# MLP1 of an attention and two-MLP kernel in blocks of 256 and 384 tokens, with the wide blocks' sums packed in three PSUM banks

## The chip, the cores and the metric

The kernel runs on one core of a Trainium2 chip. The metric is the device time of one execution in microseconds (us), lower is better. The engines are named as in the profile: PE is TensorE (matmuls), PEld its weight loads, DVE is VectorE, ACT is ScalarE, POOL is GpSimd, SP issues the DMAs. PSUM has eight banks; one bank holds 512 fp32 values on each of 128 partitions.

## The reference

Windowed attention over 4 sequences of 576 positions (8 heads of 64), then two MLPs over all 2304 tokens (512 -> 2048 -> 512):

```
scores = scale * q @ k.T + slope_h * (-|i - j|), masked to 0 <= i - j < 128
attn   = softmax(scores) @ v
x      = attn with the heads side by side        # 2304 x 512
h = x @ w_in;  g = where(h >= 1, h, where(h <= -1, 0, (h + 1)**2 / 4));  x = g @ w_out
h = x @ w_in2; g = h * clip(h + 3, 0, 6) / 6;                            out = g @ w_out2
```

The weights come as 64-bit floats. slope_h is 2 to the power -(h + 1), scale is 1/8.

## The kernel before

**Numbers in two parts.** Each fp32 operand of a matmul is split in a high part (`split_hi`) and a remainder (`split_lo`), and a product is three matmuls (low x high, high x low, high x high) in `fp32r`. Every matmul names its stationary operand, and the trace has one weight load on PEld for each matmul.

**Attention.** The tokens are cut in `units`: (256, 320) for the first, third and fourth sequence, (192, 256, 128) for the second. A head of a unit is prepared once (`prep`: high and low part of k, q and v, with the 128 keys before the unit), and each 128 queries of it are a step with four stages (`stage_a` scores and exponential, `stage_b` transposes, `stage_c` the product with v, `stage_d` for the first three units). `tick` runs one stage of several steps. There are 160 steps, eight heads times 20, and 164 ticks. In a step the scores go to bank s, the transposes to t and t2 in turn, the product with v to r.

**MLP1** runs in nine blocks of 256 tokens. For each of 16 slices f of d_ff, `Mlp.first` makes h (12 matmuls with 256 columns), `activate` makes g in two parts (DVE, ACT, DVE, ACT, POOL), and `Mlp1.second` adds g times w_out to the sum (12 matmuls with 256 columns). The sum of a block, four pieces of 128 x 256, fills two banks (acc0, acc1). `Chunks.run` keeps `lag` slices between first and second: two, and four (`LAG_TAIL`) for the last two blocks. The first two blocks run in halves of 8 slices, in the order first half of 0, first half of 1, second half of 0, second half of 1. The hook of `spread` puts the ticks of attention between the slices: 20 before MLP1, 44 within blocks 0 and 1, then 12, 24, 24, 16 and 24 in blocks 2 to 6. So attention ends with block 6. Blocks 7 and 8 run in turns slice by slice (`tail_hook`), while the second MLP's weights are loaded and converted (`Weights.conv1` to `conv3`: two ACT passes, three DVE passes, one ACT copy, one DVE subtraction, each of 128 x 1024). A block's sum leaves PSUM in `finish`, and goes to x2d in HBM.

**MLP2** takes two blocks of 384 tokens in turns and then three of 512. Its `second` has 512 columns in a matmul, whatever the block.

**Order.** The queues of SP are in the order of the program. On the other engines a scheduler sets the order, close to that of the program; each engine executes its own queue in order.

**Start.** `make_consts` builds a distance table and a mask on POOL, and `make_bias` one bias table of 128 x 256 for each of the eight heads on DVE. In the first three units a column of ones beside v gives the softmax sum; POOL writes those ones (L258) again for every pair of heads, after the last reader of that buffer. `keep_busy` puts matmuls on zeros between the first steps, to keep PE active.

Of the kernel before, what the change touches and what calls it, by code (L numbers as in the profile page):

```python
# [39 lines left out]
def tile_window_attention_two_mlps(  # L40
# [28 lines left out]
    N1 = 256  # L69
    blocks1 = [(a, min(N1, NT - a)) for a in range(0, NT, N1)]  # L70
# [13 lines left out]
    assert needs[:3] == [1, 2, 3]  # L84

# [11 lines left out]
    def keep_busy(bank, n):  # L97


        nc.tensor.matmul(bank[:, :n], zeros[:, :P], zeros[:, :n], start=True, stop=True, skip_group_check=True)  # L100

    rel_mask = []

    def make_consts():
        both = cpool.tile([P, 2, PIECE], F32, tag="m", name="both")
        irel, mask = both[:, 0, :2 * P], both[:, 1, :2 * P]
        rel_mask.extend((irel, mask))

        nc.gpsimd.iota(irel, pattern=[[-1, 2 * P]], base=P, channel_multiplier=1,
                       allow_small_or_imprecise_dtypes=True)  # L110
        nc.gpsimd.memset(mask, 0.0)
        nc.gpsimd.affine_select(out=mask, in_=mask, compare_op=ALU.is_ge, fill=NEG / scale,
                                base=P, pattern=[[-1, 2 * P]], channel_multiplier=1)
        nc.gpsimd.affine_select(out=mask, in_=mask, compare_op=ALU.is_ge, fill=NEG / scale,
                                base=WINDOW - 1 - P, pattern=[[1, 2 * P]], channel_multiplier=-1)
        make_identity(nc, ident)

    def make_bias(h):
        nc.vector.scalar_tensor_tensor(out=bias8[:, h, :], in0=rel_mask[0], scalar=-slopes[h] / scale,
                                       in1=rel_mask[1], op0=ALU.mult, op1=ALU.add)  # L120
# [116 lines left out]
    class Attention:  # L237
# [4 lines left out]

        def load(self, n):
# [40 lines left out]
        def prep(self, n):  # L284
# [27 lines left out]

        def stage_a(self, n, i):

            u = heads[n]
            if n < H and i == 0:
                make_bias(n)
# [9 lines left out]
            if u.whole:  # L327
                keep_busy(ps, BANK if u.unit == 0 else 2 * P)
            nc.tensor.matmul(ps[:m, :nk], u.qs[:, qo:qo + m], u.kh[:, ko:ko + nk], start=True, stop=False)  # L329
            nc.tensor.matmul(ps[:m, :nk], u.qs[:, qo:qo + m], u.kl[:, ko:ko + nk], start=False, stop=True)  # L330
# [4 lines left out]
                out=pt[:m, :nk], in0=ps[:m, :nk], in1=bias8[:m, u.h, bo:bo + nk], scale=-scale,  # L335
# [10 lines left out]
        def stage_b(self, n, i):  # L346
# [10 lines left out]
            bank = psum.tile([P, BANK], F32, tag=("t", "t2")[(n * 3 + i) % 2], name=f"t{n}_{i}")  # L357
# [113 lines left out]
        def to_x(self, u, xf, e_lo):  # L471
            a, end = u.t0, u.t0 + u.nq
            while a < end:
                blk = a // N1
                e = min(end, (blk + 1) * N1)
                src = xf[:, a - u.t0:e - u.t0]
                hi, lo = (self.xs[blk][:, p, u.h // 2, a - blk * N1:e - blk * N1] for p in range(2))
                split_hi(HI["x"], hi, src)
                split_lo(e_lo, lo, src, hi)
                a = e  # L480
# [62 lines left out]
    class Mlp1(Mlp):  # L543
        acc_tags = [("acc0", "acc1")]
        n_block = 0
        lag = LAG

        def accs(self, n):
            tags = self.acc_tags[self.n_block % len(self.acc_tags)]
            self.n_block += 1  # L550
            return [psum.tile([P, BANK], F32, tag=tags[i], name=f"acc{i}") for i in range(-(-KC * n // BANK))]
# [12 lines left out]
        def second(self, acc, g, f, n, first, last):  # L564

            per = BANK // n
            for e in range(KC):
                i, o = divmod(e, per)
                for k, (a, b) in enumerate(((1, 0), (0, 1), (0, 0))):
                    nc.tensor.matmul(acc[i][:, o * n:(o + 1) * n], self.W.w_out(a, f)[:, e * P:(e + 1) * P], g[:, b, :n],  # L570
                                     start=(first and k == 0 and o == 0), stop=(last and k == 2),
                                     skip_group_check=True)
# [12 lines left out]
        def finish(self, acc, t0, n, more):  # L585

            m = BANK // n * n
            o = self.left if more else self.opool.tile([P, 2, PIECE], F32, tag="m", name="o1")
            for i, (ps, hbm) in enumerate(zip(acc, self.places(acc, t0, n))):
                if more:  # L590
                    nc.vector.tensor_tensor(out=o[:, i, :m], in0=ps[:, :m], in1=o[:, i, :m], op=ALU.add)
                else:
                    split_hi(("act", "dve")[i % 2], o[:, i, :m], ps[:, :m])
                nc.sync.dma_start(out=hbm, in_=o[:, i, :m].rearrange("p (e t) -> p e t", t=n))

    class Mlp2(Mlp):
        g_lo = "g2"
        banks = ("acc0", "acc1", "r", "s", "t", "t2")
# [72 lines left out]
    def split_x2(pool, xs, j, c, raw):  # L671
# [16 lines left out]
    halves = {}  # L688
    W1 = Weights("a", w_in1, w_out1, cpool)
# [14 lines left out]
    def run_block(mlp1, j, part, hook):  # L704
        for f in part:
            chunks.run(mlp1, j, f, part, xs[j], lambda: hook(f, 0), lambda: hook(f, 1))

    with ExitStack() as actx:
        mlp1 = Mlp1(W1, blocks1, actx.enter_context(tc.tile_pool(name="r", bufs=2)),
                    actx.enter_context(tc.tile_pool(name="g", bufs=LAG + 1)))  # L710
# [15 lines left out]
        new_x(1)
# [8 lines left out]

        new_x(2)
# [21 lines left out]
        new_x(3)  # L758
        run_block(mlp1, 1, Z, spread(Z, 4, KF))
        for j in range(2, len(blocks1) - 2):  # L760
            new_x(j + 2)
# [5 lines left out]
    chunks.flush()  # L767
    opool = ctx.enter_context(tc.tile_pool(name="o", bufs=5))
# [100 lines left out]
```

## Time and profile before

| | us |
|---|---|
| three timed runs | 1011.0, 1012.44, 1012.46 (median 1012.44) |
| the profiled execution | 1012.21 |
| its span, first to last instruction | 1010.4 |
| PE busy | 981.5 |
| DVE, ACT, POOL busy | 600.4, 520.1, 250.4 |

The last matmul of MLP1 is followed by the first of MLP2 at 609.88 us of the span. A matmul's record runs from its start to a modelled end, and the records of neighbours overlap. The pace is therefore read from start to start, and the mean of a record is longer than the step. A span of 1010.4 within 1012.21 leaves 1.8 us ahead of the first and behind the last instruction.

### The profile page before, as it was taken

How to read it: one execution, taken by the hardware profiler on the slowest of the kernel's cores; microseconds unless marked ns; L12 is line 12 of the kernel's file. 1: busy time of each engine (PE TensorE's matmuls, PEld its weight loads, DVE VectorE, ACT ScalarE, POOL GpSimd, SP SyncE). 2: the span in 40 equal slices, each digit the busy share in tenths (PEclk: the TensorE clock that was granted, in tenths of full speed). 3: DMA queues.
4: the chain of work that ended last, by engine and by line, in shares of the span. 5: the costliest groups of instructions: out<-in, count | busy, mean ns of one | idle time of the engine just before them, and what ended most of it. 6: DMA issues, size and time to landing. Idle time of an engine off the chain costs nothing.

```text
span 1010.4 us, 18091 instructions
## 1 busy us (share of the span) xinstructions
PE 981.5 (97%) x6454; PEld 889.2 (88%) x6454; DVE 600.4 (59%) x1584; ACT 520.1 (51%) x1286; POOL 250.4 (25%) x398
## 2 busy tenths in 40 slices
PE   7899999999899999999999999999999999999998
PEld 4678888999899999999999998999988888888886
DVE  5789996576687776677658987922242223222222
ACT  4678885455677766666636867422232223122221
POOL 4325464444556555555400000000000000000000
PEclk9799999999999999999999999999999999999999
DMA  6575823212222212212006655000020002001001
GB/s 179 165 219 172 263 80 100 77 54 54 82 75 78 79 46 71 68 54 75 2 22 209 222 181 202 1 1 1 1 104 1 1 1 84 1 0 42 1 1 42
DMA packets 69786, 78.52 MB, mean 78 GB/s; under 512 B 7488, under 2 KB 61760, under 8 KB 69696
## 3 DMA queue, kind: packets, MB, share of 16 engines
q1 hardware_dynamic: 69696, 77.36, 24.7%
q8 instruction: 51, 0.84, 0.3%
q14 instruction: 39, 0.32, 0.1%
HBM read 66.85 MB, written 10.49 MB: 77 GB/s over the span
## 4 chain that ended last, share of the span: by engine, by line
PE 83%; DVE 5%; DMA 3%; ACT 3%; issue 3%; POOL 1%; SPq 1%; ACTq 0%; POOLq 0%; DVEq 0%
PE h L530 36%; PE acc L623 20%; PE acc L570 17%; PE r L449 2%; PE s L329 2%; PE t L363 1%; PE s L330 1%; PE t L364 1%; PE r L394 1%; DMA kr<-kT 1%; DMA rawa<-w_out 1%; DVE ma L179 1%; DVE wa L134 1%; SPq L251 1%; DVE p L334 1%
## 5 line engine op out<-in xcount | busy, mean ns | idle before, releaser
L530 PE MATMUL h<-x,wa 128*128 128x256 f32 x1728 | 240.6, 286 | 2.4 <-DVE sm L340 1.3
L570 PE MATMUL acc<-g,wa 128*128 128x256 f32 x1728 | 236.6, 285 | 1.4 <-POOL g L134 1.3
L530 PEld LDWEIGHTS h<-x,wa 128*128 128x128 f32 x1728 | 220.3, 192 | 4.0 <-DVE sm L340 1.5
L570 PEld LDWEIGHTS acc<-g,wa 128*128 128x128 f32 x1728 | 217.9, 191 | 3.4 <-POOL g L134 1.8
L530 PE MATMUL h<-x,wb 128*128 128x512 f32 (+1 forms) x960 | 210.5, 368 | 1.2 <-DVE r L613 1.2
L623 PE MATMUL acc<-wb,g 128*128 128x512 f32 x864 | 209.4, 390 | 0.0
L530 PEld LDWEIGHTS h<-x,wb 128*128 128x128 f32 x960 | 176.2, 188 | 26.5 <-DVE r L613 1.5
L623 PEld LDWEIGHTS acc<-wb,g 128*128 128x128 f32 x864 | 161.7, 188 | 32.4
L613 DVE SCALAR_TENSOR_TENSOR r<-r,h 128x512 f32<-128x512 f32 (+1 forms) x80 | 50.7, 633 | 203.4 <-ACT r L612 203.4
L612 ACT ACTIVATE r<-h 128x512 f32<-128x512 f32 (+1 forms) x80 | 44.4, 555 | 211.5 <-PE h L530 211.4
L127 ACT CAST g<-r 128x256 fp32r<-128x256 f32 (+2 forms) x224 | 104.4, 466 | 86.1 <-DVE r L613 50.1
L134 POOL TENSOR_TENSOR g<-r,g 128x256 fp32r<-128x256 f32 x112 | 88.9, 794 | 129.9 <-ACT g L127 122.5
L558 ACT ACTIVATE r<-r 128x256 f32<-128x256 f32 x144 | 60.1, 417 | 78.8 <-DVE r L557 75.3
L134 DVE TENSOR_TENSOR g<-r,g 128x512 fp32r<-128x512 f32 (+2 forms) x112 | 64.5, 576 | 46.6 <-ACT g L127 46.5
L337 ACT ACTIVATE p<-p,sm 128x256 f32<-128x256 f32 (+2 forms) x160 | 76.1, 477 | 23.0 <-DVE sm L334 19.8
L559 DVE TENSOR_TENSOR r<-h,r 128x256 f32<-128x256 f32 x144 | 60.6, 421 | 29.9 <-ACT r L558 28.8
L557 DVE TENSOR_SCALAR r<-h 128x256 f32<-128x256 f32 x144 | 60.4, 419 | 28.8 <-PE h L530 24.0
L134 POOL TENSOR_TENSOR qs<-qr,qs 64x256 fp32r<-64x256 f32 (+3 forms) x72 | 66.5, 924 | 28.7 <-issue 10.8
L334 DVE CUSTOM_DVE_ANT_0 p<-s,bias 128x256 f32<-128x256 f32 (+2 forms) x160 | 59.8, 374 | 13.1 <-PE s L330 12.3
L329 PE MATMUL s<-kh,qs 128*128 128x256 f32 (+2 forms) x160 | 56.7, 356 | 5.0 <-POOL qs L134 3.6
L342 POOL TENSOR_SCALAR p<-p,sm 128x256 f32<-128x256 f32 (+2 forms) x104 | 48.0, 461 | 54.4 <-DVE sm L341 35.2
L376 DVE TENSOR_TENSOR tl<-t,th 128x256 fp32r<-128x256 f32 (+2 forms) x120 | 41.7, 348 | 11.7 <-ACT th L127 10.3
(75 smaller groups left out, 1124.5 us busy)
## 6 DMA issues: line engine op xcount, KB each, us to landing
rawa<-w_in SPq DMA_DIRECT2D x16, 512.0 KB, 5.2
rawa<-w_out SPq DMA_DIRECT2D x16, 512.0 KB, 4.8
rawb<-w_in SPq DMA_DIRECT2D x16, 512.0 KB, 3.7
rawb<-w_out SPq DMA_DIRECT2D x16, 512.0 KB, 4.7
x2d<-o SPq DMA_DIRECT2D x22, 256.0 KB, 2.5
kr<-kT SPq DMA_DIRECT2D x48, 112.0 KB, 2.6
out<-o SPq DMA_DIRECT2D x18, 256.0 KB, 2.1
kr<-kT SPq DMA_DIRECT2D x64, 64.0 KB, 2.3
```

The source lines that it names most:

```text
L127: nc.scalar.copy(hi, x)
L134: engines[eng].tensor_tensor(out=lo, in0=x, in1=hi.bitcast(F32), op=ALU.subtract)
L329: nc.tensor.matmul(ps[:m, :nk], u.qs[:, qo:qo + m], u.kh[:, ko:ko + nk], start=True, stop=False)
L334: nc.vector.tensor_tensor_reduce(out=pt[:m, :nk], in0=ps[:m, :nk], in1=bias8[:m, u.h, bo:bo + nk], scale=-scale, scalar=3.0e38, op0=ALU.ad ...
L337: nc.scalar.activation(out=pt[:m, :nk], in_=pt[:m, :nk], func=AF.Exp, bias=sm[:m, 0:1], scale=-1.0, accum_out=None if u.whole else sm[:m, ...
L530: nc.tensor.matmul(ps[:, :n], self.W.w_in(a, c, f), self.x_chunk(x, b, c, n), start=(k == 0), stop=(k == 3 * KC - 1))
L557: nc.vector.tensor_scalar(out=r[:, :n], in0=ps[:, :n], scalar1=-1.0, scalar2=1.0, op0=ALU.max, op1=ALU.min)
L558: nc.scalar.activation(out=r[:, :n], in_=r[:, :n], func=AF.Square, bias=0.5, scale=0.5)
L559: nc.vector.tensor_tensor(out=r[:, :n], in0=ps[:, :n], in1=r[:, :n], op=ALU.max)
L570: nc.tensor.matmul(acc[i][:, o * n:(o + 1) * n], self.W.w_out(a, f)[:, e * P:(e + 1) * P], g[:, b, :n], start=(first and k == 0 and o == 0 ...
L613: nc.vector.scalar_tensor_tensor(out=r[:, :n], in0=r[:, :n], scalar=1.0, in1=ps[:, :n], op0=ALU.min, op1=ALU.mult)
L623: nc.tensor.matmul(acc[t][:, :DM], g[:, b, t * P:(t + 1) * P], self.W.w_out(a, f), start=(first and k == 0), stop=(last and k == 2))
```

## The change

- MLP1: three blocks of 256 and then four of 384 tokens. The sum of a block of 384 is four pieces of 128 x 384, and a bank takes one such piece and 128 columns more. In blocks 3 to 5 (`packed`) the fourth piece is cut in three of 128 columns, one behind the piece in each of three banks (acc0, acc1, t2). So its 3 matmuls are 9 in each slice.
- The last block (6) is alone, without packing: four banks (s, t, acc0, acc1) for the sum, h0 and r for h, with a lag of two slices. The `flush` ahead of it and ahead of MLP2 is gone.
- Attention: (256, 320), (192, 256, 128), (256, 128, 192), (192, 256, 128). Steps stay 160, but the heads are 88 instead of 72. The ticks are 20, 24, 32 and 24 in blocks 2 to 5. From the fourth block's units on the transposes use bank t alone.
- The x of MLP1 is one tile in two halves with a place for each block, instead of three buffers.
- One table of distances for all heads: k is scaled by scale / slope_h in `prep`, and the slope comes in with the minimum on DVE. The 8 DVE instructions of `make_bias` go.
- The ones beside v are written once, ahead of all loads. ACT writes one column of the zeros at the start, which loads its function table then. `keep_busy` uses matmuls of 256 columns.
- The conversion of the second weights is spread differently (0.5 a slice of the last block, then 0.6 a slice of each MLP2 block).

```diff
-    N1 = 256
-    blocks1 = [(a, min(N1, NT - a)) for a in range(0, NT, N1)]
+    N1, WIDE = 256, 384
+    assert (NT - 3 * N1) % WIDE == 0
+    blocks1 = [(a, N1) for a in range(0, 3 * N1, N1)] + [(a, WIDE) for a in range(3 * N1, NT, WIDE)]
...
-        for n in (192, 256, 128) if b == 1 else (256, 320):
+        for n in ((256, 320), (192, 256, 128), (256, 128, 192), (192, 256, 128))[b]:
...
+            unit = scale / slopes[u.h]
+            assert math.frexp(unit)[0] == 0.5
+            nc.scalar.activation(out=u.kh[:, :nk], in_=u.kr[:, :nk], func=AF.Copy, scale=unit)
...
+            nc.vector.scalar_tensor_tensor(out=u.kl[:, :nk], in0=u.kr[:, :nk], scalar=unit,
+                                           in1=u.kh[:, :nk].bitcast(F32), op0=ALU.mult, op1=ALU.subtract)
...
-            bank = psum.tile([P, BANK], F32, tag=("t", "t2")[(n * 3 + i) % 2], name=f"t{n}_{i}")
+            bank = psum.tile([P, BANK], F32, tag=("t", "t2")[(n * 3 + i) % 2] if u.unit <= first_wide else "t",
+                             name=f"t{n}_{i}")
...
+        acc_tags = ("acc0", "acc1", "t2")
+        packed = True
...
+            return [psum.tile([P, BANK], F32, tag=self.acc_tags[i], name=f"acc{i}")
+                    for i in range(-(-KC // (BANK // n)) - (self.packed and n == WIDE))]
...
             per = BANK // n
             for e in range(KC):
-                i, o = divmod(e, per)
+                if e == len(acc) and per == 1:
+
+                    pieces = [(i, n, i * P, P) for i in range(n // P)]
+                else:
+                    pieces = [(e // per, e % per * n, 0, n)]
                 for k, (a, b) in enumerate(((1, 0), (0, 1), (0, 0))):
...
+                    for i, o, t, m in pieces:
+                        nc.tensor.matmul(acc[i][:, o:o + m], self.W.w_out(a, f)[:, e * P:(e + 1) * P],
+                                         g[:, b, t:t + m], start=(first and k == 0 and o == 0),
+                                         stop=(last and k == 2), skip_group_check=True)
...
-    chunks.flush()
-    opool = ctx.enter_context(tc.tile_pool(name="o", bufs=5))
...
+    mlp1.tags = ("h0", "r")
+    mlp1.acc_tags = ("s", "t", "acc0", "acc1")
+    mlp1.packed = False
...
     for f in FULL:
-        chunks.run(mlp1, y, f, FULL, xs[y], lambda: None, tail_hook(f, False))
-        chunks.run(mlp1, z, f, FULL, xs[z], lambda: None, tail_hook(f, True))
-    chunks.flush()
-    for f in range(KF - behind, KF):
-        W2.load()
-        W2.load()
...
+        chunks.run(mlp1, z, f, FULL, z, lambda: None, lambda: tail_hook(f))
```

Three places show how the instructions move. The first is PE in a slice whose sum was 2 banks before (top), and in a packed slice of block 3 (below); h is the product with w_in, acc the sum, wa the weights of MLP1:

```order
L530 MATMUL h<-x,wa_1363 128x256 x12
L570 MATMUL acc_3061<-g,wa_1119 128x256 x6
L570 MATMUL acc_3062<-g,wa_1119 128x256 x6
L449 MATMUL r_3353<-th_3225,vs_2750 128x128
L449 MATMUL r_3353<-tl_3226,vs_2750 128x128
```

```order
L549 MATMUL h<-x,wa_776 128x384 x12
L598 MATMUL acc_4313<-g,wa_647 128x384 x3
L598 MATMUL acc_4314<-g,wa_647 128x384 x3
L598 MATMUL acc_4315<-g,wa_647 128x384 x3
L598 MATMUL acc_4313<-g,wa_647 128x128
L598 MATMUL acc_4314<-g,wa_647 128x128
L598 MATMUL acc_4315<-g,wa_647 128x128
L598 MATMUL acc_4313<-g,wa_647 128x128
L598 MATMUL acc_4314<-g,wa_647 128x128
L598 MATMUL acc_4315<-g,wa_647 128x128
L598 MATMUL acc_4313<-g,wa_647 128x128
```

(two more rows of 128 columns follow.) The fourth piece of the sum has become nine matmuls of 128 columns in a row.

The second is PE where MLP1 hands over to MLP2 (x_0 and x_1 are the first two blocks of MLP2, wb its weights), before and then now:

```order
L570 MATMUL acc_8491<-g,wa_2233 128x256 x6
L570 MATMUL acc_8492<-g,wa_2233 128x256 x6
L530 MATMUL h<-x_0_0_8647,wb_8725 128x384 x3
L530 MATMUL h<-x_0_1_8719,wb_8725 128x384 x3
L530 MATMUL h<-x_0_2_8800,wb_8725 128x384 x3
L530 MATMUL h<-x_0_3_8881,wb_8725 128x384 x3
L530 MATMUL h<-x_1_0_8953,wb_8725 128x384 x3
```

```order
L549 MATMUL h<-x_0_3_8753,wb_8710 128x384 x3
L598 MATMUL acc_8530<-g,wa_2167 128x384 x3
L598 MATMUL acc_8531<-g,wa_2167 128x384 x3
L598 MATMUL acc_8532<-g,wa_2167 128x384 x3
L598 MATMUL acc_8533<-g,wa_2167 128x384 x3
L549 MATMUL h<-x_1_0_8793,wb_8710 128x384 x3
L549 MATMUL h<-x_1_1_8842,wb_8710 128x384 x3
```

The last two slices of MLP1's sum now stand between the first slices of MLP2. 

The third is ACT's queue at the start (kh is k's high part, p the exponential, th the transposed p; 151/167 is head 0, 176/190 head 1), before and then now:

```order
L127 CAST kh_151<-kr_119 128x256
L127 CAST kh_176<-kr_128 128x256
L127 CAST kh_211<-kr_158 128x256
L337 ACTIVATE p_0_172<-p_0_172,sm_0_173 128x128
L337 ACTIVATE p_1_194<-p_1_194,sm_1_195 128x256
```

```order
L303 ACTIVATE kh_167<-kr_152 128x256
L353 ACTIVATE p_0_186<-p_0_186,sm_0_187 128x128
L353 ACTIVATE p_1_209<-p_1_209,sm_1_210 128x256
L137 COPY th_213<-t_0_214 128x128
L137 COPY th_213<-t_1_235 128x256
L303 ACTIVATE kh_190<-kr_159 128x256
```

Head 1's k now stands behind all of head 0's work on ACT.

## Rows read from the trace of the kernel before

**Rows 1.** The page: busy time of each engine, share of the span, instructions.

```profile
PE 981.5 (97%) x6454; PEld 889.2 (88%) x6454; DVE 600.4 (59%) x1584; ACT 520.1 (51%) x1286; POOL 250.4 (25%) x398
```

**Rows 2.** Stretches by stage: length, each engine's busy us (instructions), PEclk, DMA share, GB/s.

```profile
28.40:101.80 73.40, 66.11 (x453) 55.03 (x453) 63.19 (x157) 58.34 (x132) 28.51 (x36) 0.94 0.61 186
197.20:252.50 55.30, 55.30 (x471) 55.30 (x470) 37.15 (x117) 31.55 (x94) 25.06 (x42) 1.00 0.19 50
252.50:322.50 70.00, 65.22 (x539) 63.12 (x538) 54.98 (x207) 49.71 (x166) 41.52 (x73) 1.00 0.30 85
322.50:390.70 68.20, 67.78 (x546) 64.79 (x545) 48.71 (x195) 45.72 (x152) 36.86 (x62) 1.00 0.20 55
390.70:447.00 56.30, 56.17 (x476) 55.82 (x475) 40.16 (x145) 35.51 (x114) 30.29 (x51) 1.00 0.26 74
447.00:517.70 70.70, 69.65 (x558) 66.43 (x557) 44.53 (x170) 41.99 (x135) 30.40 (x51) 1.00 0.10 29
517.70:609.90 92.20, 92.20 (x771) 92.20 (x770) 76.20 (x142) 60.19 (x106) 0.00 (x0) 1.00 0.55 185
609.90:1010.40 400.50, 395.44 (x1826) 337.28 (x1824) 141.74 (x209) 119.55 (x200) 0.00 (x0) 1.00 0.08 28
```

**Rows 3.** Timeline of PE without attention, MLP1: start, length, line, count.

```profile
599.80 1.60 PE L570 MATMUL acc<-g,wa 128*128 128x256 f32 x12
601.24 1.60 PE L530 MATMUL h<-x,wa 128*128 128x256 f32 x12
```

**Rows 4.** The same in MLP2's blocks of 384 tokens.

```profile
695.12 2.27 PE L530 MATMUL h<-x,wb 128*128 128x384 f32 x12
697.22 2.24 PE L623 MATMUL acc<-wb,g 128*128 128x512 f32 x9
```

**Rows 5.** Timeline of PE: four matmuls of 128 columns in a row.

```profile
253.90 0.22 PE L449 MATMUL r<-th,vs 128*128 128x128 f32 x1
253.96 0.27 PE L449 MATMUL r<-tl,vs 128*128 128x128 f32 x1
254.07 0.28 PE L449 MATMUL r<-th,vs 128*128 128x128 f32 x1
254.18 0.28 PE L449 MATMUL r<-tl,vs 128*128 128x128 f32 x1
254.30 0.29 PE L363 MATMUL t<-ident,p 128*128 128x128 f32 x1
```

**Rows 6.** Timeline of PEld: the weight loads of the last two of those.

```profile
254.01 0.19 PEld L449 LDWEIGHTS r<-th,vs 128*128 128x128 f32 x1
254.12 0.19 PEld L449 LDWEIGHTS r<-tl,vs 128*128 128x128 f32 x1
```

**Rows 7.** Timeline of PE where MLP2 begins.

```profile
609.88 4.33 PE L530 MATMUL h<-x,wb 128*128 128x384 f32 x24
615.40 2.38 PE L530 MATMUL h<-x,wb 128*128 128x384 f32 x12 [1.20 <-DVE r L613]
```

**Rows 8.** Waits from 0 to 171.2 us: who for whom, us, times, longest.

```profile
POOL vr L258 <- PE r L394: 14.7, 9, 3.2
PE s L329 <- POOL qs L134: 3.6, 4, 1.4
```

**Rows 9.** Timeline of ACT at the start.

```profile
6.73 0.41 ACT L127 CAST kh<-kr 128x256 fp32r<-128x256 f32 x1 [1.39 <-DMA kr<-kT]
11.09 0.40 ACT L127 CAST kh<-kr 128x256 fp32r<-128x256 f32 x1 [3.95 <-DVE sm L334]
```

**Rows 10.** DVE by line and shape, whole span: count, then busy us, mean ns, idle before.

```profile
L175 DVE TENSOR_SCALAR mb<-mb 128x1024 uint32<-128x1024 uint32 x16 | 10.7, 687 | 2.0 <-ACT mb L168 2.0
L177 DVE SCALAR_TENSOR_TENSOR mb<-rawb,mb 128x1024 uint32<-128x1024 uint32 x16 | 19.5, 1218 | 0.0
L134 DVE TENSOR_TENSOR wb<-mb,wb 128x1024 fp32r<-128x1024 f32 x16 | 19.5, 1220 | 3.1 <-ACT wb L127 3.1
L134 DVE TENSOR_TENSOR g<-r,g 128x384 fp32r<-128x384 f32 x32 | 17.8, 557 | 12.5 <-ACT g L127 12.5
```

More of the change, by code (lines that the diff above doesn't have):

```diff
@@ L97, in keep_busy @@
     def keep_busy(bank, n):
-        nc.tensor.matmul(bank[:, :n], zeros[:, :P], zeros[:, :n], start=True, stop=True, skip_group_check=True)
-    rel_mask = []
+        for a in range(0, n, 2 * P):
+            nc.tensor.matmul(bank[:, a:a + 2 * P], zeros[:, :P], zeros, start=True, stop=True, skip_group_check=True)
     def make_consts():
[L105 to L109, printed above, removed]
+        rel = cpool.tile([P, 2, PIECE], F32, tag="m", name="rel")[:, 0, :2 * P]
+        nc.gpsimd.iota(rel, pattern=[[1, 2 * P]], base=-P, channel_multiplier=-1,
                        allow_small_or_imprecise_dtypes=True)
-        nc.gpsimd.memset(mask, 0.0)
-        nc.gpsimd.affine_select(out=mask, in_=mask, compare_op=ALU.is_ge, fill=NEG / scale,
+        nc.gpsimd.affine_select(out=rel, in_=rel, compare_op=ALU.is_ge, fill=NEG / min(slopes),
                                 base=P, pattern=[[-1, 2 * P]], channel_multiplier=1)
[L114 to L120, printed above, removed]
+        last = nc.gpsimd.affine_select(out=rel, in_=rel, compare_op=ALU.is_ge, fill=NEG / min(slopes),
+                                       base=WINDOW - 1 - P, pattern=[[1, 2 * P]], channel_multiplier=-1)
+        with tc.issue_after(last.ins):
+            make_identity(nc, ident)
+        nc.vector.tensor_copy(dist, rel)
     engines = {"act": nc.scalar, "dve": nc.vector, "pool": nc.gpsimd, "any": nc.any}
@@ L241, in __init__ @@
             self.k_owners, self.v_owners = [], []
+            self.vts = [raw.tile([P, KCH, 2 * D + 2], F32, tag="vr", name=f"vr{i}") for i in range(2)]
         def load(self, n):
@@ L311, in prep, with scores @@
                 u.vs = heads[n - 1].vs
+        def scores(self, u, ps, qo, ko, m, nk):
+            parts = [(u.qs, u.kh), (u.qs, u.kl)]
+            for w, (q, k) in enumerate(parts):
+                nc.tensor.matmul(ps[:m, :nk], q[:, qo:qo + m], k[:, ko:ko + nk],
+                                 start=(w == 0), stop=(w == len(parts) - 1))
         def stage_a(self, n, i):
             u = heads[n]
-            if n < H and i == 0:
-                make_bias(n)
             a, m = u.qbs[i]
@@ L688, in tile_window_attention_two_mlps @@
     halves = {}
+    thirds = [0, 1, 2]
     W1 = Weights("a", w_in1, w_out1, cpool)
@@ L781, in tile_window_attention_two_mlps @@
     xs2 = {}
-    y, z = len(blocks1) - 2, len(blocks1) - 1
-    behind = LAG_TAIL // 2
+    state = [0.0]
     def conv2(rate):
@@ L822, in tile_window_attention_two_mlps @@
     pair.close()
+    scope1.close()
+    opool = ctx.enter_context(tc.tile_pool(name="o", bufs=5))
     xpool2 = ctx.enter_context(tc.tile_pool(name="xb", bufs=3))
```

147 lines of the change are left out of this document (76 added, 71 removed).

## The prediction

> **What bounds the kernel now.** First the busy times: PE is busy for 981.5 of 1010.4 us, every other engine for less than two thirds [rows 1]. Then the stretches by stage [rows 2], because an average mixes stages. MLP2 (400.5 us) and the last two blocks of MLP1 (92.2 us) have PE at its pace: a block of 256 without attention is 16 slices of 24 matmuls, 2 x 1.44 us a slice by the starts 599.80 and 601.24 [rows 3], so 0.120 us a matmul and 46.1 us a block, and two blocks make the 92.2 us. In blocks 2 to 6 attention stands between the slices. Their lengths are 55.3, 70.0, 68.2, 56.3 and 70.7 us with 12, 24, 24, 16 and 24 ticks. Less 46.1 us, block 2 leaves 0.77 us a tick and block 5 0.64. In these two PE is never idle [rows 2], so I take 0.70 as the price of a tick on PE. Blocks 3, 4 and 6 then have 208.9 - 138.2 - 72 x 0.70 = 20.3 us that are neither: lost in waits, 0.28 us a tick. Up to 171 us the program is bound by its chains of attention and conversion: from 28.4 to 101.8 us DVE is busy for 63.2 of 73.4 us and PE has only 453 matmuls [rows 2]. So MLP1 from block 2 on, 197.2 to 609.9 us, is the stretch that the change remakes, and there PE's pace and the lost time count. The granted clock is 1.00 in all of it (2.4 GHz).
>
> **The change part by part.** *Wide matmuls.* In MLP2's blocks of 384, 12 matmuls of 384 columns take 2.10 us by the starts 695.12 and 697.22 [rows 4]: 0.175 us each, against 0.120 for 256. For the same tokens two wide ones (0.350) replace three narrow ones (0.360). That is all there is to win on PE, 2.8%. Over 1536 tokens: six blocks cost 6 x 384 x 0.120 = 276.5 us; four unpacked ones would cost 4 x 384 x 0.175 = 268.8.
>
> *The packed piece.* In blocks 3 to 5 each slice has nine matmuls of 128 columns where three of 384 would stand, in all 432. What do they cost? The nearest row is L449: four of 128 columns in a row, of the same kind, in pairs with the same stationary operand. Their starts are 253.90, 253.96, 254.07, 254.18, and the next is at 254.30: the second seems to come after 0.06 us, but it lasts longer (0.27 against 0.22), and from then on the step is 0.11 [rows 5]. Under them PEld loads a stationary operand for each, at the same steps of 0.11 (254.01, 254.12) [rows 6]. So a narrow matmul is bound by its weight load, also where the stationary operand is the one before, and 0.11 us is my value; the lower bound is the 0.06 step, the upper one the 0.12 of a matmul of 256. A packed slice is then 12 x 0.175 + 9 x 0.175 + 9 x 0.11 = 4.67 us, a packed block 74.6 us; an unpacked one is 24 x 0.175 x 16 = 67.2. Sum for the 1536 tokens: 3 x 74.6 + 67.2 = 291.0 us, **14.5 us more than before**. The packing costs 22 us and the wider matmul gives 8.
>
> *Attention.* The ticks stay 100 from block 2 on: 70 us at 0.70. Units of 128 and 192 make more heads; the counts of L449 go from 128 to 192 of 128 columns and from 80 to 48 of 256, so 64 x 0.11 - 32 x 0.12 = 3.3 us more. 16 more preparations fall to ACT, DVE and POOL, which are idle for a third of the time in these blocks and more [rows 2], so I give them no price of their own.
>
> *The lost time.* It depends on how densely ticks stand. Without loss a tick came every (46.1 + 16.8) / 24 = 2.62 us in blocks 3, 4 and 6 (0.28 us lost in each), and every (46.1 + 11.2) / 16 = 3.58 us in block 5 (none). Now it is 20 ticks in 60.1 us in block 2 and 32 in 97.0 us in block 4, 3.0 us both, and 24 in 91.4 us in blocks 3 and 5, 3.8 us. On a line between the two points 3.0 us loses 0.16 us a tick, times 52 = 8.5 us; blocks 3 and 5 lose nothing. Bounds: 0 if the wider slices cover all, 20 if the single transpose bank and the extra heads take it back.
>
> *The last block.* The two blocks in turns were 92.2 us with nothing lost, though DVE was busy for 76.2 us of it [rows 2]. Now a slice is 4.20 us, and DVE has in it three passes over 384 columns (0.557 each: 1.67), half a conversion (0.687 + 2 x 1.218 + 1.220 = 4.34, half is 2.17; L179 is priced as L177) and in eight slices a remainder of x2 (0.557) [rows 10]: 4.40 us in 4.20. Behind a conversion pass stand DVE's two passes on h, and behind these g, which PE needs two slices later instead of four. Between 0 and 6 us (half a microsecond in each of twelve slices); I take 1, since the overdraft of 0.2 us in eight slices is 1.6 us and the scheduler mixes the passes.
>
> *The hand-over.* Now PE makes two first slices from 609.88 us, then stands until 615.40 [rows 7]; 24 x 0.175 = 4.2 us were due at 614.1. With the last two sums of MLP1 between them the wait for g is covered: 1.3 us less.
>
> *The start.* The one bias table takes 8 DVE instructions away. POOL's 14.7 us of waiting with the ones (L258) for PE ends, but PE itself waited only 3.6 us for q from POOL [rows 8]: at most 3.6 us less. Against it, head 1's k, made at 6.73 us before, now queues on ACT behind head 0's exponential and transposes, where head 2's k (11.09) and more stood [rows 9]: up to 2 us more. I take 1 us less, from 4 less to 2 more.
>
> **Sum.** 197.2 to 609.9 us was 412.7. Now: 46.1 (block 2) + 291.0 + 70 + 3.3 + 8.5 + 1 = 419.9, so 7.2 more; less 1.3 and 1.0 gives 4.9. MLP2 has the same matmuls. The profiled execution took 1012.21 us, its span 1010.4; the median of the runs is 1012.44, so the execution stands for them. 1012.2 + 4.9 = **1017.1 us**. About 0.2% (2 us) is what a measurement of this kernel can tell from no change.
>
> **Rivals.** *The wide blocks cover all the waits (not slower).* In the stretch from 197 us, the price of a tick could be block 5's 0.64, so 24.6 us were lost in blocks 3, 4 and 6, and a slice of 4.67 us gives attention's chains time enough: 46.1 + 291.0 + 64 + 3.3 = 404.4, 8.3 less; with the 2.3 of hand-over and start, 1001.6 us. It decides where the losses (8.5 + 1 in my sum) fall below about 6.5 us: then it is no longer slower, and below 2.5 it is faster. For it: block 5 at 3.6 us a tick loses nothing. Against it: block 2, at 3.0 us, has the eight single-step heads with which block 3 lost most (4.8 us of PE idle in 65.2 of 70.0 [rows 2]).
>
> *The narrow matmuls are cheap.* If a second and third piece with the same stationary operand followed after 0.06 us, as 253.96 after 253.90 [rows 5], the 432 would cost 21.6 us less: 995.5 us. Against it are the steps of 0.11 behind, and PEld's loads.
> The Trainium skill, TensorE: Matmul & The Clock Gate, section "Back-to-back issue gap", gives about 81 ns for a stream of loads and matmuls with 128 columns (and 131 ns with 512). By that the 432 would cost 12.5 us less, and the sum would be 1004.6 us. The trace's own steps (0.11, and nine of 512 columns in a record of 2.24 us) differ from both figures, so I give it no more than a share of this rival's chance.
>
> *The losses stay.* The single bank t, eight heads per unit of 128 in three units, and the last block behind the conversions: 20 us lost in blocks 2 to 5 and 6 in the last, so 16.5 us more than my sum: 1033.6 us. For it: DVE is already at 79% in block 3. Against it: ticks are rarer.
>
> **How the numbers follow.** My case 0.66 (of it 0.10 within 2 us of no change), all waits covered 0.14 (0.09 faster, 0.05 no change), cheap narrow matmuls 0.08 (faster), losses stay 0.12 (slower). Faster 0.17, same 0.15, slower 0.68. The range of 8 in 10 is 1005 to 1029: down into the covered case, up to half of the losses that stay, with the bounds of the start and of 0.12 a narrow matmul (4 us) within it.
>
> **What would show it.** Right: the nine narrow matmuls of a slice start 0.11 us apart and a packed slice without attention takes 4.6 to 4.7 us; blocks 3 to 5 together take 280 to 300 us; the last block 67 to 70; no gap at the first slices of MLP2. Wrong: steps near 0.06; PE idle above 10 us in blocks 2 to 5 or in the last block, then the losses stayed; a first MLP1 matmul more than 4 us away from 28.4 us, then the start was misjudged.

## The result, and the profile after

The changed kernel takes 1017.22 us (median of 13 runs, 1015.34 to 1026.34), the kernel before beside it 1012.46 us (13 runs): a ratio of 1.0051, 95% interval 1.0031 to 1.0072. It is slower by 4.8 us. The prediction said 1017.1. The profiled execution took 1017.27 us with a span of 1014.9 (before: 1012.21 and 1010.4). The page's busy times, to be read against [rows 1]:

```profile
PE 991.6 (98%) x6036; PEld 906.4 (89%) x6036; DVE 597.0 (59%) x1541; ACT 516.6 (51%) x1260; POOL 260.1 (26%) x403
```

PE has 418 instructions fewer and is busy for 10 us longer. The stretches by stage from block 2 on (block 2, block 3, 4, 5, the last block, MLP2; columns as in [rows 2]):

```profile
195.60:259.80 64.20, 63.42 (x534) 62.39 (x533) 50.33 (x180) 44.59 (x144) 35.74 (x63) 1.00 0.26 70
259.80:349.10 89.30, 89.30 (x623) 88.99 (x622) 62.33 (x211) 54.02 (x168) 46.04 (x77) 1.00 0.24 64
349.10:451.40 102.30, 100.92 (x682) 96.69 (x682) 65.08 (x270) 60.24 (x208) 52.59 (x92) 1.00 0.21 59
451.40:544.20 92.80, 92.80 (x647) 92.80 (x646) 58.69 (x183) 49.41 (x145) 39.62 (x60) 1.00 0.16 43
544.20:611.80 67.60, 67.60 (x398) 67.60 (x398) 53.30 (x80) 44.76 (x66) 1.01 (x1) 1.00 0.69 237
611.80:1014.90 403.10, 399.29 (x1850) 341.56 (x1848) 153.31 (x224) 127.88 (x209) 0.00 (x0) 1.00 0.09 30
```

Blocks 3 to 5 take 284.4 us, and PE stands idle in them for 1.4 (102.30 - 100.92 in block 4). The timeline of PE in a packed slice without attention (start, length, line, shape of the first, count; the 18 are nine matmuls of 384 and nine of 128 columns), and then PE's groups of the sum by shape (count, busy us, mean ns):

```profile
344.46 2.31 PE L549 MATMUL h<-x,wa 128*128 128x384 f32 x12
346.62 2.68 PE L598 MATMUL acc<-g,wa 128*128 128x384 f32 x18
349.13 0.39 PE L549 MATMUL h<-x,wa 128*128 128x384 f32 x1
```

```profile
L598 PE MATMUL acc<-g,wa 128*128 128x384 f32 x624 | 120.0, 337 | 0.0
L598 PE MATMUL acc<-g,wa 128*128 128x128 f32 x432 | 53.6, 269 | 0.0
```

From 344.46 to 349.13 it is 4.67 us, 2.51 of it for the sum. The hand-over, where [rows 7] had a gap of 1.20 us:

```profile
609.76 2.24 PE L598 MATMUL acc<-g,wa 128*128 128x384 f32 x12
611.84 2.24 PE L549 MATMUL h<-x,wb 128*128 128x384 f32 x12
613.92 2.24 PE L598 MATMUL acc<-g,wa 128*128 128x384 f32 x12
616.00 2.24 PE L549 MATMUL h<-x,wb 128*128 128x384 f32 x12
618.08 2.24 PE L598 MATMUL acc<-g,wa 128*128 128x384 f32 x12
620.16 2.24 PE L549 MATMUL h<-x,wb 128*128 128x384 f32 x12
622.24 2.24 PE L657 MATMUL acc<-wb,g 128*128 128x512 f32 x9
```

The starts lie 2.08 us apart with no gap, and two sums of MLP1 (4.2 us) stand inside MLP2's stretch. Counting these to MLP1 (611.84 + 4.16 = 616.0), the profile adds up so:

| part | predicted | from the two profiles |
|---|---|---|
| up to block 2 | -1.0 | -1.7 (block 2 begins at 195.6, before at 197.2) |
| MLP1 from block 2 on | +7.2 | +7.8 (195.6 to 616.0 is 420.4 us, before 412.7) |
| hand-over and MLP2 | -1.3 | -1.6 (398.9 us, before 400.5) |
| span | +4.9 | +4.5 |

### The profile page after: what moved, and what is told of

It is laid out like the page before. It is cut to its first block, busy times and chain, and to the rows that moved or that the text cites. A ratio compares the mean times of both kernels' runs of the same rounds, so it can differ in the third digit from the quotient of the medians.

```text
span 1014.9 us, 17405 instructions
## 1 busy us (share of the span) xinstructions
PE 991.6 (98%) x6036; PEld 906.4 (89%) x6036; DVE 597.0 (59%) x1541; ACT 516.6 (51%) x1260; POOL 260.1 (26%) x403
## 4 chain that ended last, share of the span: by engine, by line
PE 84%; DVE 5%; DMA 4%; ACT 3%; issue 1%; SPq 1%; POOL 1%; POOLq 0%; ACTq 0%; DVEq 0%
PE h L549 37%; PE acc L657 19%; PE acc L598 19%; PE r L466 3%; PE s L329 3%; DMA qr<-qT 2%; PE t L380 1%; PE t L381 1%; PE r L411 1%; DMA rawa<-w_out 1%; SPq L263 1%; ACT p L353 1%; DVE ma L189 1%; DVE r L579 1%; DVE p L350 1%
## 5 line engine op out<-in xcount | busy, mean ns | idle before, releaser
L598 PE MATMUL acc<-g,wa 128*128 128x384 f32 (+2 forms) x1632 | 249.7, 301 | 1.9 <-POOL g L144 1.8
L549 PE MATMUL h<-x,wa 128*128 128x384 f32 (+1 forms) x1344 | 232.1, 317 | 1.9 <-DVE wa L144 1.1
L137 ACT CAST g<-r 128x384 fp32r<-128x384 f32 (+2 forms) x192 | 98.2, 512 | 72.7 <-DVE r L647 50.8
L144 POOL TENSOR_TENSOR g<-r,g 128x256 fp32r<-128x256 f32 (+1 forms) x96 | 92.4, 962 | 134.9 <-ACT g L137 116.9
L580 ACT ACTIVATE r<-r 128x384 f32<-128x384 f32 (+1 forms) x112 | 53.5, 478 | 100.0 <-DVE r L579 99.9
L144 DVE TENSOR_TENSOR g<-r,g 128x384 fp32r<-128x384 f32 (+1 forms) x96 | 59.9, 624 | 45.9 <-ACT g L137 45.7
L579 DVE TENSOR_SCALAR r<-h 128x384 f32<-128x384 f32 (+1 forms) x112 | 55.6, 496 | 44.4 <-PE h L549 37.5
L581 DVE TENSOR_TENSOR r<-h,r 128x384 f32<-128x384 f32 (+1 forms) x112 | 55.7, 497 | 29.6 <-ACT r L580 28.9
L350 DVE CUSTOM_DVE_ANT_0 p<-s,dist 128x256 f32<-128x256 f32 (+2 forms) x160 | 59.8, 375 | 16.6 <-PE s L329 14.3
L305 DVE SCALAR_TENSOR_TENSOR kl<-kr,kh 128x256 fp32r<-128x256 f32 (+4 forms) x88 | 49.0, 557 | 7.3 <-ACT kh L303 7.1
```

Of the source, the lines that this page charges most:

```text
L137: nc.scalar.copy(hi, x)
L144: engines[eng].tensor_tensor(out=lo, in0=x, in1=hi.bitcast(F32), op=ALU.subtract)
L350: nc.vector.tensor_tensor_reduce(out=pt[:m, :nk], in0=ps[:m, :nk], in1=dist[:m, bo:bo + nk], scale=-slopes[u.h], scalar=3.0e38, op0=ALU.ad ...
L549: nc.tensor.matmul(ps[:, :n], self.W.w_in(a, c, f), self.x_chunk(x, b, c, n), start=(k == 0), stop=(k == 3 * KC - 1))
L579: nc.vector.tensor_scalar(out=r[:, :n], in0=ps[:, :n], scalar1=-1.0, scalar2=1.0, op0=ALU.max, op1=ALU.min)
L580: nc.scalar.activation(out=r[:, :n], in_=r[:, :n], func=AF.Square, bias=0.5, scale=0.5)
```

## The experiments

The theory was the prediction's sum: the packed sum's narrow matmuls cost 0.11 us each on PE, which outweighs the wide ones' gain, and attention's waits depend on how densely its ticks stand. The rival: a narrow matmul costs 0.06 us, and what the kernel loses it loses in waits (the one transpose bank, more heads) or in the opening. All runs are of the changed kernel with one edit, where nothing else is said. Lengths of stages are from the profiled executions.

### What a narrow matmul costs

The first kernel packs nothing and gives the fourth sum a bank of its own, which it takes from h:

```diff
-        acc_tags = ("acc0", "acc1", "t2")
-        packed = True
+        acc_tags = ("acc0", "acc1", "t2", "h1")
+        packed = False
...
+            if j == first_wide:
+                mlp1.tags = ("h0",)
```

> The changed kernel, but blocks 3 to 5 have no packing: the sum takes four banks (acc0, acc1, t2 and h1), and h has the single bank h0 in these blocks. 432 matmuls of 128 columns become 144 of 384. Theory (a narrow matmul costs its weight load, 0.11 us): PE's work falls by 432 x 0.11 - 144 x 0.175 = 22.3 us; against it the single h bank: DVE's two passes and ACT's one on h (3 x 0.55 us, and their queues) must end within the second matmuls and the ticks (2.1 + about 1 us a slice). If they do, 995 us; with 0.15 us lost in each of 48 slices 1002. Rival (narrow matmuls cost 0.06 us): PE gains 0.7 us only, and the single bank makes it 1017 to 1025 us.

Measured: 1000.3 us (median of 4 runs), 0.9882 of the kernel before (0.9858 to 0.9907). It beats both kernels. Its blocks 3, 4 and 5, and what PE waited for most in them (us in all, times, longest):

```profile
259.90:344.20 84.30, 83.27 (x539) 82.28 (x538) 62.98 (x211) 53.65 (x167) 45.68 (x77) 1.00 0.26 67
344.20:443.70 99.50, 94.28 (x587) 88.92 (x585) 68.11 (x271) 60.30 (x208) 51.78 (x92) 1.00 0.22 60
443.70:529.60 85.90, 85.34 (x549) 85.03 (x549) 59.73 (x184) 48.88 (x145) 39.09 (x60) 1.00 0.18 47
```

```profile
PE h L549 <- DVE r L581: 2.5, 4, 0.9
PE t L381 <- DVE sm L356: 2.3, 4, 0.7
PE t L380 <- DVE sm L356: 1.3, 2, 0.7
```

The three blocks take 269.7 us, 14.7 less than packed. By the pace alone (4.20 for 4.67 us in 48 slices) it should have been 22.6 less (23.5 by the last block's 4.16 us a slice and the 46 packed sums that stand in these stretches; the sums run two slices behind). So 8 to 9 us came back, and PE's idle time rose from 1.4 to 6.8 us (1.0, 5.2 and 0.6 in the three rows). Where they came from is the question of the next section.

The second kernel leaves six of the nine narrow matmuls out in all slices but a block's first and last:

```diff
-                    for i, o, t, m in pieces:
+                    for i, o, t, m in pieces if first or last else pieces[:1]:
```

> The changed kernel, but in the 14 middle slices of blocks 3 to 5 two of each three narrow matmuls are left out (two thirds of the fourth piece of the sum are wrong): 252 matmuls of 128 columns less, nothing else. This prices one. Theory (0.11 us, bound by the weight load, though the stationary operand is the same for all three): blocks 3 to 5 are 27.7 us shorter. Rival (same stationary operand, 0.06 us): 15 us shorter.

Measured: 999.99 us (one run), span 998.1, which is 16.8 less. At face value that speaks for the rival's 0.06 us. The timeline of a slice without attention speaks otherwise:

```profile
341.32 2.33 PE L549 MATMUL h<-x,wa 128*128 128x384 f32 x12
343.49 2.00 PE L598 MATMUL acc<-g,wa 128*128 128x384 f32 x12
345.33 0.40 PE L549 MATMUL h<-x,wa 128*128 128x384 f32 x1
```

The sum of nine wide and three narrow ones takes 1.84 us where 18 took 2.51: 0.67 us for six, 0.11 each, and 42 such slices make the expected 28 us. Blocks 3 to 5, though, are only 20.9 us shorter (263.5 us), since PE is idle in them for 5.8 us, most of it ahead of attention's transposes (t), which wait for DVE (the second fence):

```profile
263.20:345.30 82.10, 81.67 (x545) 80.81 (x544) 62.85 (x211) 53.57 (x167) 45.94 (x78) 1.00 0.26 69
345.30:443.10 97.80, 92.42 (x598) 87.38 (x598) 68.09 (x270) 59.85 (x206) 51.77 (x92) 1.00 0.23 60
443.10:526.80 83.70, 83.70 (x563) 83.66 (x562) 59.38 (x185) 49.82 (x145) 39.75 (x61) 1.00 0.19 50
```

```profile
PE t L381 <- DVE sm L356: 3.2, 4, 1.0
PE t L380 <- DVE sm L356: 1.5, 2, 0.8
```

The rest of the way to 16.8 is block 2 (0.5 us longer), the last block (0.7) and the opening: block 2 began at 198.56 instead of 195.56 us, for which the edit is no cause (see the end of this part). The price stands, but the span alone would have told the wrong story.

The third kernel puts a wide and a narrow matmul in turns, so that a narrow one is never followed by another:

```diff
+                for k, (a, b) in enumerate(((1, 0), (0, 1), (0, 0))):
+                    for i in range(n // P):
+                        for e, o, t, m in ((i, 0, 0, n), (KC - 1, n, i * P, P)):
...
```

> The changed kernel, but a packed slice issues wide and narrow matmuls in turns (384 columns into a bank, then 128 columns into the same bank) instead of nine narrow ones in a row; same work, same count. Theory A (only one weight load runs ahead, so a narrow matmul makes its successor wait for a whole load wherever it stands): no change, a packed slice stays at 4.67 us, 1017 us. Theory B (the time that the wide matmul leaves over its successor's load, 0.175 - 0.11, can be used by the load after): a pair costs max(0.175 + 0.06, 2 x 0.11) = 0.235 instead of 0.285 us, 0.45 us less a slice, 48 slices: 22 us less, 995 us.

Measured: 1018.52 us, 1.0062 of before (1.0042 to 1.0081), no different from the changed kernel. The slice:

```profile
345.23 2.30 PE L549 MATMUL h<-x,wa 128*128 128x384 f32 x12
347.37 2.70 PE L594 MATMUL acc<-g,wa 128*128 128x384 f32 x18
349.90 0.39 PE L549 MATMUL h<-x,wa 128*128 128x384 f32 x1
```

4.67 us again (345.23 to 349.90). So a narrow matmul costs its 0.11 us wherever it stands. That it is a weight load that shows in it is read from PEld's equal steps [rows 6]; no run changed the loads alone. PEld has a load for each matmul, also for one that repeats its operand (in blocks 3 to 5 of the changed kernel 852 loads of the sum, 414 of them for narrow ones). The Trainium skill, TensorE: Matmul & The Clock Gate, section "LDWEIGHTS (loading the stationary operand)", gives columns / 1.2 ns for a load; for 128 columns that would be 107 ns, an estimate from the page with which the step of 0.11 us agrees. The 81 ns that the prediction quoted from the section "Back-to-back issue gap" is not what these streams show (0.11 us).

### Where the waits come from

The line of the prediction (lost time against the spacing of ticks) is tried in the kernel before itself, with 20 ticks in each of blocks 2 to 6 in place of 12, 24, 24, 16, 24:

```diff
-            ticks = sum(unit_steps[:needs[j + 1]]) + LAG_D - att.t
+            ticks = 20
```

> The kernel before, with 20 ticks in each of blocks 2 to 6 instead of 12, 24, 24, 16, 24; nothing else. My line on lost time: 20.3 us lost before; a tick every (46.1 + 14) / 20 = 3.0 us loses 0.16 us, 100 of them 16 us: 4 us less, 1008 us. Rival (what is lost belongs to the single-step heads of the 128-token unit, not to the density): within 2 us of 1012.4.

Measured: 1006.8 us, 0.9946 of before (0.9925 to 0.9966), with no instruction added or taken away. Blocks 2 to 6, against the rows of [rows 2]:

```profile
197.10:261.10 64.00, 63.17 (x534) 62.28 (x533) 50.47 (x180) 44.54 (x144) 35.70 (x64) 1.00 0.27 70
261.10:320.80 59.70, 59.58 (x501) 58.82 (x500) 46.02 (x169) 40.81 (x133) 34.36 (x57) 1.00 0.28 77
320.80:384.40 63.60, 63.60 (x520) 61.64 (x519) 44.36 (x171) 41.03 (x134) 33.62 (x56) 1.00 0.19 53
384.40:444.80 60.40, 59.82 (x502) 59.01 (x501) 46.44 (x169) 40.37 (x132) 33.65 (x56) 1.00 0.28 76
444.80:510.10 65.30, 65.30 (x531) 63.26 (x531) 39.95 (x146) 36.95 (x117) 27.29 (x45) 1.00 0.08 25
```

They take 313.0 us for 320.5. The same ticks, evenly spread, take 7.5 us less, where the line had 4, so the spacing is a cause.

The rival for what came back in the unpacked kernel is its single h bank. The next kernel stays packed and keeps h in one bank in blocks 3 to 5:

```diff
+            if j == first_wide:
+                mlp1.tags = ("h0",)
```

> The changed kernel as it is (packed slices), but h only in bank h0 in the wide blocks 3 to 5, as e1_one_h has it. e1_one_h's blocks 3 to 5 took 269.7 us, where the slice's pace alone (4.20 in place of 4.67 us, 48 slices) would have made 284.4 - 22.6 = 261.8 us: 7.9 us came back as waits. Theory 'the waits come from the shorter slice, since attention's chains need their time between two ticks': here the slices keep their 4.67 us, so blocks 3 to 5 stay at 284.4 +- 1.5 us. Rival 'the waits come from the single h bank': blocks 3 to 5 take 288 to 293 us, and the weight loads and matmuls of h wait for DVE's r (L581) there.

Measured: 1017.85 us (one run); blocks 3 to 5 take 285.3 us (the first of them below), 0.9 more than with two banks. The single h bank is not where the 8 us come from while the slices are long. The second kernel above, which has two h banks, says the same from the other side: it too gave back 7 of its 28 us. With short slices the bank has a part: 2.5 of the unpacked kernel's 6.8 us of idle time stand ahead of h, where the second kernel waits for nothing.

```profile
259.30:349.20 89.90, 89.60 (x623) 89.15 (x623) 62.46 (x211) 54.05 (x168) 45.87 (x77) 1.00 0.24 64
```

If a chain of attention is too slow for the shorter slices, more ticks between its steps should help. Two kernels, built on the unpacked one, try it: one puts the transposes a tick later, the other the products with v too.

```diff
-LAG_B, LAG_C, LAG_C_SPLIT, LAG_D = 2, 3, 4, 4
+LAG_B, LAG_B_SPLIT, LAG_C, LAG_C_SPLIT, LAG_D = 2, 3, 3, 4, 4
...
+                                      (LAG_C_SPLIT, False, self.stage_c), (LAG_B_SPLIT, False, self.stage_b),
+                                      (LAG_B, True, self.stage_b)):
```

(Also: in the second, LAG_C_SPLIT is 5, which puts one tick more in block 2; in both, p has one buffer more, and xf has one in place of two.)

> e1_one_h with the transposes of a step one tick later (three ticks behind its scores in place of two, from unit 3 on; the products with v stay four ticks behind), xf with one buffer for the room. In e1_one_h PE stands idle for 6.8 us in blocks 3 to 5, most of it with the transposes in front, which wait for DVE's and POOL's passes on p (sm, L356; 3.6 us of PE's idle time) and with h (2.5 us). Theory 'the waits that came back are the chain scores-exponential-p, which has two ticks of time and needs more where ticks come every 2.7 us': the transposes wait no more, PE's idle time in blocks 3 to 5 falls to 2 to 4 us, blocks 3 to 5 take 264 to 267 us in place of 269.7, median 995 to 998 us. Rival 'PE is behind the engines' work as a whole, or the one t bank': the wait moves to the products with v (for th and tl) or to h, and blocks 3 to 5 stay at 269 to 271 us, median 1000 +- 1.5 us.

> e10_later_transposes with the products with v one tick later too (five ticks behind the scores), so that the copies of the transposes keep their two ticks; attention then ends one tick later in each block. Theory 'time between the ticks': as e10_later_transposes or up to 2 us better (blocks 3 to 5 in 263 to 266 us, median 994 to 997 us), the more so if e10's products with v wait. Rival 'the one t bank or the engines as a whole': blocks 3 to 5 at 269 to 271 us again, median 1000 to 1002 us, since a tick is added.

Measured: 999.56 us (0.9876 of before, 0.9843 to 0.9909) and 1006.02 us (0.9932, 0.9913 to 0.9952). Of the first, block 4, and in the second fence all that PE waited for in blocks 3 to 5; in the third, all that PE waited for in block 2 of the second kernel (this profiled execution took 1013.52 us, more than the median):

```profile
341.90:439.70 97.80, 97.64 (x587) 90.15 (x585) 68.14 (x273) 60.49 (x208) 51.53 (x92) 1.00 0.23 61
```

```profile
PE h L550 <- DVE r L582: 1.2, 2, 0.7
```

```profile
PE r L466 <- DVE xf L484: 4.7, 4, 2.0
```

With later transposes the wait for sm is gone, and PE's idle time falls from 6.8 to 1.4 us, as the theory had it. The blocks, though, fall only from 269.7 to 267.3 us, just short of the expected range, and the median does not differ from the unpacked kernel's, as the rival had it. So the chain to p accounts for some 2 of the 8 us. Of the remainder, some 3 us sit where PE counts as busy, in attention's own matmuls: from start to start they take 65.1 us in blocks 3 to 5, for 61.9 in the changed kernel. In block 4 it is now 0.21 us from a step's last product with v to the transpose behind it, where it was 0.13 to 0.15. Other shapes stand beside each other there; why these steps are longer stays open. A fifth tick of lag costs more than it gives: 1006.02 us is more than either expectation had. Block 2 alone takes 70.6 us there, with one tick more, for 64.2 (64.6 in the first kernel), since the next pair's products wait until DVE has read the one r bank. Blocks 3 to 5 take 271.7 us in this execution; the granted clock in block 3 was 0.98, so they settle little.

### What the extra heads cost

The kernel before with the changed kernel's units, and its own 12, 24, 24, 16 and 24 ticks:

```diff
-        for n in (192, 256, 128) if b == 1 else (256, 320):
+        for n in ((256, 320), (192, 256, 128), (256, 128, 192), (192, 256, 128))[b]:
...
+            ticks = (12, 24, 24, 16, 24)[j - 2]
```

> The kernel before, with the units of the changed kernel, (256, 128, 192) and (192, 256, 128) in the last two sequences, and the ticks of blocks 2 to 6 held at 12, 24, 24, 16, 24. So 88 heads instead of 72 in the same steps. Theory: 3.3 us more of PE's work and some lost time (24 ticks in a block of 256 with single-step heads): 1015 to 1020 us. Rival (the 16 preparations are free and the heads only rearrange): within 2 us of 1012.4.

Measured: 1018.98 us, 1.0058 of before (1.0035 to 1.0080). Blocks 2 to 6 take 327.3 us (195.7 to 523.0) for 320.5: 6.8 us for 16 heads, where the prediction's matmuls make 3.3. The other half is waits. What PE waited for most from block 3 to block 6, here and, in the second fence, before:

```profile
PE r L449 <- DVE xf L467: 5.3, 9, 1.4
```

```profile
PE r L449 <- DVE xf L467: 2.4, 2, 1.9
```

A pair of short heads asks for the one r bank sooner than DVE has read it. The opposite edit, in the unpacked kernel, joins two units to one of 384, eight heads fewer:

```diff
-        for n in ((256, 320), (192, 256, 128), (256, 128, 192), (192, 256, 128))[b]:
+        for n in ((256, 320), (192, 256, 128), (384, 192), (192, 256, 128))[b]:
```

> The kernel of e1_one_h (nothing packed, four sums in four banks, one h bank), with one unit of 384 tokens in place of one of 256 and one of 128 (units 6 and 7), so eight heads fewer and the same 24 ticks in block 3; xf has one buffer, for the room. The runs so far: 24 more heads' preparations and narrower matmuls in a kernel of 256-blocks (e4_before_more_heads) made the blocks 2 to 6 6.8 us longer for 16 more heads, 0.43 us a head. Theory 'a head has its price on PE and in waits': block 3, where eight heads fall away, goes from 84.3 us to 81 to 82.5 us, the rest stays within 1 us, median about 997.5 us. Rival 'the tick sets the price, whatever number of heads': block 3 stays at 84.3 +- 0.7 us and the time at 1000.3 +- 1.5. Rival 'the one xf buffer is waited for': block 3 or 4 longer than before by more than 1 us.

Measured: 998.87 us, 0.9856 of before (0.9812 to 0.9901), within the uncertainty of the unpacked kernel. Block 3:

```profile
259.80:343.00 83.20, 81.83 (x523) 80.56 (x522) 56.21 (x188) 48.01 (x137) 40.13 (x62) 1.00 0.18 50
```

1.1 us less than 84.3, between the two expectations: of the products with v, 32 of 128 columns fall away and 16 of 256 are added (1.6 us less at 0.11 and 0.12), and some of that is idle time now (1.4 for 1.0 us). The waits of the kernel before did not come off with the heads here. Eight heads are 0.14 us each here, 16 were 0.43 each in the kernel before, so these runs show no single price for a head.

### The hand-over and the opening

One line puts the two last sums of MLP1 ahead of MLP2 again:

```diff
+    chunks.flush()
```

> The changed kernel, with the flush of MLP1's last two slices put back ahead of MLP2. Theory: the gap in front of MLP2's third group of first matmuls returns, 1.2 to 1.3 us of PE idle, as in the kernel before; the span is 1.3 us longer. Rival (the wider last block or the lag of two slices hides it): no gap, no change.

Measured: 1018.94 us (one run), span 1017.2. PE where MLP2 begins:

```profile
610.20 6.40 PE L598 MATMUL acc<-g,wa 128*128 128x384 f32 x36
616.44 4.33 PE L549 MATMUL h<-x,wb 128*128 128x384 f32 x24
621.39 3.06 PE L549 MATMUL h<-x,wb 128*128 128x384 f32 x16 [0.63 <-DVE r L647]
625.17 2.31 PE L657 MATMUL acc<-wb,g 128*128 128x512 f32 x9 [0.72 <-DVE g L144]
```

The idle time is 0.63 + 0.72 = 1.35 us, as expected, though half of it stands ahead of MLP2's first sum. From its first matmul to the end of the span MLP2 takes 400.8 us (616.44 to 1017.2), with MLP1's sums in between, and these taken out, 398.9: 1.9 us. The last block and MLP2 together are 3.4 us longer; the other 1.5 stand ahead of the flush, where PE waited for 0.6 us in all. What the rest is isn't settled.

The last kernel lets POOL write the ones for each pair again:

```diff
+                if u.whole:
+                    nc.gpsimd.memset(u.vt[:, :, 0:2 * D + 2:2 * D + 1], 1.0)
...
-        for vt in att.vts:
-            nc.gpsimd.memset(vt[:, :, 0:2 * D + 2:2 * D + 1], 1.0)
```

> The changed kernel, with POOL writing the ones beside v again for every pair of heads in the first three units, as before. Theory (the 1.7 us that blocks 0 and 1 came earlier are POOL's freed queue): block 2 begins 1 to 3 us later than 195.6 us. Rival (they are the eight bias tables that DVE no longer makes, or the order): it begins within 0.7 us of 195.6.

Measured: 1020.09 us (one run). POOL waits again for PE with the ones:

```profile
POOL vr L269 <- PE r L413: 26.0, 9, 4.8
```

PE's own wait for q from POOL in the first 29 us is 2.1 us, for 1.2 in the changed kernel. Block 2 begins at 196.95 us, where the theory had 196.6 to 198.6. But that settles nothing: in the seven kernels whose code up to there is the changed kernel's own it begins at 194.3 to 198.6 us, and in the three with the opening of before at 195.7 to 197.2. The opening varies by more than the edit.

## Why the prediction was right, point by point

**The narrow matmuls** were the core, and they held: 4.67 us a packed slice, 0.11 us a matmul by leaving six out of nine, and no change in turns. The rival of 0.06 us falls. That the median comes within 0.1 us of the forecast is luck: the interval of the ratio leaves 3 to 7 us, and two terms of the sum are off by more than 2 us in opposite directions.

**The packing costs 22 us, the wider matmul gives 8** is right as PE's pace, but not as what undoing it brings. Undone, blocks 3 to 5 gave 14.7 us. The narrow matmuls were also time in which attention's chains went on.

**The lost time** was mis-sized, twice, and the errors nearly cancel. The term that was off is "blocks 3, 4 and 6 then have 208.9 - 138.2 - 72 x 0.70 = 20.3 us". At the end of block 6 of the kernel before the timeline has

```profile
513.27 4.61 PE L570 MATMUL acc<-g,wa 128*128 128x256 f32 x36
```

36 matmuls of the sum, not 12: a flush adds two slices' sums (2.9 us) to that block, which I counted as waits. So 17.4 us were lost, 0.24 a tick, not 0.28. The changed kernel has no flush there, but block 2 still begins with two sums of block 1, so the same 2.9 us were missing from my sum. Its true loss is 420.4 - 46.1 - 291.0 - 70 - 3.3 - 2.9 = 7.1 us, where I had 8.5 + 1. With 0.24 at its dense end the line gives 0.14 a tick at 3.0 us, 7.3 us over 52 ticks, so here it held, once the flush's 2.9 us are taken out of it. The place agrees too: less MLP1's matmuls and 0.70 a tick, blocks 2 to 5 leave 4.1, 0.0, 5.2 and 1.3 us (the extra heads' matmuls within them), most in the two blocks with ticks at 3.0 us. The kernel before with even ticks has 313.0 - 230.5 - 70 - 2.9 = 9.6 us over 100 ticks at the same 3.0 us: 0.10 a tick where my line gave 0.16. That spacing rules was right; two points were too few to say how much it costs in another kernel.

**The last block** loses nothing: 16 slices of h and 14 sums at 2.08 us and two packed sums of 2.51 make 67.4, and it took 67.6. DVE's overdraft of 0.2 us in eight slices, for which I had put 1 us, is covered: DVE is busy for 53.3 us of the stretch.

**The extra heads** were put at 3.3 us "with no price of their own" for preparations. In the kernel before they cost 6.8, the rest in waits for the r bank. In the changed kernel, with its rarer ticks, the loss of 7.1 us has room for little of that.

**The hand-over** gave 1.6 us by the profiles for 1.3 predicted, and 1.9 when it was undone. **The start** can't be called right: the profiles differ by 1.7 us, less than the opening varies.

Of the rivals, "the wide blocks cover all the waits" came nearest, since the loss is smaller than my line said, but 7.1 us were lost on top of 0.70 a tick, where it needed less than about 6.5 to be no slower and less than 2.5 to be faster. "The losses stay" (20 us) falls by the 7.1.

## What to carry to other kernels

Price a matmul by the larger of its own step and that of the weight loads, as the trace has them (0.175 us at 384 columns; 0.11 at 128, where the loads come every 0.11): splitting a wide piece into narrow ones to save a PSUM bank cost 22 us of PE time here, and a kernel that gave up the second bank of h instead was 17 us faster. A saving on the bounding engine is not paid out in full where a second chain runs in its shadow: 22.6 us became 14.7 and 28 became 21, so look at the idle time after each such step. Spreading the same background work evenly over the stages gained 6 us without one instruction more.

## What the runs showed of the hardware that was not expected

A narrow matmul's wait need not show at its successor. In turns, the starts in blocks 3 to 5 are 0.228 us from a wide to a narrow one and 0.06 from this to the next wide one; in a row it is 0.175 and 0.11 (medians). The pair costs 0.29 us either way. Of the steps between the nine in a row, too, one is 0.06 and the others are 0.11, as in [rows 5]: a single short step is no price.

The opening of the same code took from 28.8 to 31.5 us until MLP1's first matmul (seven kernels), and the granted clock differed too. From 20 to 28 and 28 to 32 us, first the changed kernel (first matmul at 29.2), then the one with wide and narrow in turns (31.5), whose code is the same up to there:

```profile
20.00:28.00 8.00, 5.46 (x29) 4.12 (x27) 6.69 (x15) 5.31 (x12) 3.09 (x4) 0.79 0.77 228
28.00:32.00 4.00, 2.82 (x24) 2.38 (x23) 2.97 (x5) 3.88 (x8) 1.96 (x3) 1.00 0.62 172
```

```profile
20.00:28.00 8.00, 6.08 (x33) 4.79 (x33) 7.19 (x18) 6.32 (x13) 3.62 (x4) 0.71 0.70 202
28.00:32.00 4.00, 4.00 (x24) 3.86 (x24) 2.68 (x7) 3.12 (x8) 1.13 (x2) 0.58 0.52 128
```

In the last four microseconds the first has 2.4 GHz throughout and stands idle for 1.2 us, the second has a mean clock of 0.58, so 1.2 GHz for most of them, and is never idle. In the eight ahead PE was busy for 5.5 and 6.1 us, with gaps in both, and the mean clock was 0.79 and 0.71. In these two the clock goes the same way as the length, but it is not the whole of it: three other executions with the same mean clock of 0.83 from 12 to 32 us had their first matmul at 28.8, 30.3 and 30.5 us. That the clock is a cause wasn't tried. Which execution gets which clock is not in the code, so a term of 1 us in this opening can't be read from one profile of each kernel.
